# Retention attention and a SwiGLU block on one core: which queue stores the weight sums, and where their first groups stand

## The chip, the cores and the metric

The kernel runs on one core of one Trainium2 chip. The time is device time in microseconds for one execution of the whole program; the number for a kernel is the median of its runs. Engines are named as the profile names them: PE (TensorE), DVE (VectorE), ACT (ScalarE), POOL (GpSimd) and SP (SyncE). SP here only issues DMAs; ACT and POOL issue some as well, and an issuing engine spends time on each issue.

## The reference

```python
# retention attention: B=8, H=8, S=576, D=64, float32
scores = scale * np.matmul(q, k.transpose(0, 1, 3, 2))
gamma = 1.0 - 2.0 ** (-5.0 - np.arange(H, dtype=np.float32))
Dmat = np.where(rel >= 0, gamma[:, None, None] ** rel[None, :, :], 0.0)
attn = np.matmul(scores * Dmat[None, :, :, :], v)
# (B,H,S,D) -> x of 4608 tokens x 512
# SwiGLU: w_gate, w_val 512 x 1536, w_out 1536 x 512
g = x @ w_gate
out = (g * (1.0 / (1.0 + np.exp(-g))) * (x @ w_val)) @ w_out
```

## The kernel before

**Attention.** The 32 pairs of heads (`load`, `tick`) are worked through one after the other. `load(i)` fetches q, k (L282) and k, v (L287) of a pair, and `tick` computes its retention chunk by chunk, with a running state: DVE transposes qk to qT and kT (L492), ACT scales kn (L507) and qk (L489), PE multiplies (L532 to L573), ACT copies the results out (L584, L626, L656), and DVE applies the decay (L580, L590 to L608). A load is issued on SP into a rotating buffer, so its first issue waits until DVE has read the former contents (kT, L492). One pair, number 11, goes to a buffer of its own and is issued on ACT's DMA queue. Ticks are put in between the matmuls of the feed-forward part.

**Feed-forward.** The tokens are worked in tiles. The first 512 tokens (tile 0) go through plain matmuls: `up0` (L853 and L864 are its matmuls and those of `down0`; L856 takes silu on ACT, L857 multiplies on DVE), then `down0`, then `out0` (L870 stores the result). All later tiles (`up_stage(n)`, then down steps) use fast products: sums of blocks of x and of the weights are multiplied in fewer matmuls, and the products are added up again. L1183 is the matmul of the up half, L1374 that of the down half; every addition of two operands goes through one helper at L1040, on DVE or POOL; `finish` takes silu on ACT (L1197) and multiplies on DVE or POOL (L1198). The d_ff columns are taken in three quarters `qd` (NQ = 3), and each has seven sets of weights, in the order 1, 2, 6, 7, 4, 5, 3.

**Weight rounding.** The weights arrive as 64-bit numbers. ACT (L389, L390) splits them and DVE (L406, L407) puts them together to float32, half a block of columns after the other, while `up0` runs; ACT issues the loads of the next raw weights (L372).

**Weight sums for the up half.** In the stage n = 1 the sums of each set are made once. `w_sets(qd)` returns the sums (`outer_sums`, `inner_sums`, both on POOL) and `store`. The sums `new[o]` (128 partitions x 1024 float32, 512 KB) lie in one of three blocks of SBUF: sets 7 and 3 share the first, 6 and 2 the second, 1, 4 and 5 the third. PE multiplies with them there in stage 1, and they are stored to DRAM (`up_sets`, L1116) so that later tiles can fetch them. There are 21 such stores: three in `early_sums` (quarter 0, sets 1, 2 and 7, emitted in the `down0` loop), the others in `up_stage(1)`, each a few slots behind its sums. The sums of the next set of a block wait until its store has landed. The raw halves of each set are stored by SP (L1118 and L1119).

**Weight sums for the down half.** `out_sums(qd)` makes 26 sums per quarter, in groups of three stores (L954, on SP, 128 KB each). Quarters 0 and 1 are summed on POOL (L886) in six places of SBUF, which come free when a store has landed; quarter 2 on DVE. `negate(qd)` (L916, ACT) goes ahead of the first group of a quarter. Later tiles fetch these sums (L995).

**The order.** Every engine runs its instructions in the order in which the program emits them. Around the change the order is written out by hand: a list `plan` (L1442 onward) holds the calls for `up0(f)`, f = 2 to 11, and what is put between them. Behind f = 7, 10 and 11 stands `next_load(t)` (L1462), which loads the pair that is AHEAD pairs later: load(10), load(11) and so on. Behind it the groups of `out_sums` are put, by the dictionary in L1463, up to f = 7, 10 and 11. The remaining groups follow in the `down0` loop, one after each `down0(f)`. In the built program the DMAs that SP and ACT issue use eight completion semaphores in turn; each issue waits until the earlier DMA that used its semaphore has landed, whichever of the two engines issued that. POOL's DMAs have semaphores of their own.

Of the kernel before, what the change touches and what calls it, by code (L numbers as in the profile page):

```python
# [131 lines left out]
def kernel(  # L132
# [32 lines left out]
    nc = tc.nc  # L165
# [4 lines left out]
    P = 128  # L170
# [671 lines left out]
    def up0(f, chunks):  # L842

        pair = banks[2 * (f % 2) : 2 * (f % 2) + 2]
        for gv, bank in enumerate(pair):
            for c in chunks:
                w = w_up[:, f // 4, gv, f % 4, c // 2, (c % 2) * P : (c % 2 + 1) * P]
                if f == 2 or f == 3 and gv == 0:
                    for m in range(2):
                        nc.tensor.matmul(bank[:, ts(m, TB)], w, xs[0][:, c, ts(m, TB)],  # L850
                                         start=(c == 0 and m == 0), stop=(c == HP - 1), skip_group_check=True)
                    continue
                nc.tensor.matmul(bank, w, xs[0][:, c, :], start=(c == 0), stop=(c == HP - 1))  # L853
        if HP - 1 in chunks:
            s = io[:, (f % 2) * T0 : (f % 2 + 1) * T0]
            nc.scalar.activation(out=s, in_=pair[0], func=AF.Silu)  # L856
            nc.vector.tensor_tensor(out=hid0[f], in0=pair[1], in1=s, op=ALU.mult)  # L857
# [56 lines left out]
    def negate(qd):  # L914
        for n, s in enumerate((3, 5)):
            nc.scalar.mul(out=negatives[2 * qd + n], in_=w_dn[:, qd, s // 2, s % 2], mul=-1.0)  # L916
# [122 lines left out]
    def combine(eng, out, a, b, sign):  # L1039
        eng.tensor_tensor(out=out, in0=a, in1=b, op=ALU.add if sign > 0 else ALU.subtract)  # L1040
# [53 lines left out]
    def w_sets(qd):  # L1094

        up = lambda n, k: w_up[:, qd, :, 2 * n : 2 * n + 2, k, :]
        sets = {1: up(0, 0), 2: up(0, 1), 7: up(1, 0), 3: up(1, 1), 5: hid[:, qd, 2:4, 0:2], 6: hid[:, qd, 0:2, 2:4], 4: hid[:, qd, 2:4, 2:4]}
        blocks = (rest[:, x0_at + 1024 : x0_at + 2048], extra_at(1536, 1024), extra_at(0, 1024))
        new = {o: blocks[b].rearrange("p (g j x) -> p g j x", g=2, j=4) for o, b in {6: 1, 1: 2, 7: 0, 4: 2, 2: 1, 5: 2, 3: 0}.items()}

        def outer_sums(o):
            out, a, b = {5: (5, 7, 1), 6: (6, 3, 5), 7: (7, 3, 7), 4: (4, 2, 6)}[o]
            return [lambda g=g: combine(nc.gpsimd, sets[out][:, g], sets[a][:, g], sets[b][:, g], -1) for g in range(2)]

        def inner_sums(o):
            z = lambda k, m: sets[o][:, :, m, k * P : (k + 1) * P]
            to = lambda j: new[o][:, :, j]
            return [lambda: combine(nc.gpsimd, to(1), z(0, 1), z(0, 0), -1),
                    lambda: combine(nc.gpsimd, to(0), z(1, 1), z(0, 1), -1),
                    lambda: combine(nc.gpsimd, to(2), z(1, 1), to(1), -1),  # L1110
                    lambda: combine(nc.gpsimd, to(3), z(1, 0), to(2), -1)]

        def store(o, new_ones):
            dst = up_sets[qd][SETS.index(o)]
            if new_ones:
                return [lambda: nc.gpsimd.dma_start(out=dst[:, 6 * P :], in_=new[o].rearrange("p g j x -> p (g j x)"))]  # L1116
            raw = dst[:, 0 : 6 * P].rearrange("p (g x) -> p g x", g=2)
            return [lambda: nc.sync.dma_start(out=raw[:, :, P:], in_=sets[o][:, :, 0]),  # L1118
                    lambda: nc.sync.dma_start(out=raw[:, :, 0:P], in_=sets[o][:, :, 1, P:])]  # L1119

        return sets, new, outer_sums, inner_sums, store
# [313 lines left out]
    def next_load(t):  # L1435
        if t + AHEAD < NP:
            load(t + AHEAD)
# [6 lines left out]
    def round_until(i):  # L1444
        while todo and order.index(i) >= todo[0]:
            m = todo.pop(0)
            plan.extend(lambda j=j: rounding(j) for j in (2 * m, 2 * m + 1))
# [4 lines left out]
    for f in range(2, NF):  # L1452
        round_until({4: 12, 6: 13, 8: 14, 9: 15, 10: 16, 11: 17}.get(f, f + 2))
        plan.append(lambda f=f: up0(f, range(HP)))
        if f - 1 in tick_at and f < 7:
            plan.append(lambda t=tick_at[f - 1]: next_load(t))
        if f in tick_at and f > 2:
            plan.append(lambda t=tick_at[f]: tick(t, HP, FIRST))
            if tick_at[f] == HP + 1:
                plan.append(end_transposes)  # L1460
        if f in (7, 10, 11):
            plan.append(lambda t=tick_at[f]: next_load(t))  # L1462
        for _ in range({7: 3, 10: 4, 11: 3}.get(f, 0)):  # L1463
            if f >= (7, 10, NF)[groups[0][0]]:
                if f + 1 == NF and more_places:
                    plan.append(lambda places=more_places[:4]: pool_places.extend(places))
                    more_places.clear()
                if len(groups) % 9 == 0:
                    plan.append(lambda qd=groups[0][0]: negate(qd))
                plan.append(lambda group=groups.pop(0)[1]: group())  # L1470
# [87 lines left out]
```

## Time and profile before

| | |
|---|---|
| median of 3 runs | 1034.03 us (1033.91 to 1036.57) |
| profiled execution | 1034.89 us, its span 1033.2 us |
| granted TensorE clock, mean | 0.997 |
| busy | PE 1009.1, DVE 727.6, POOL 557.4, ACT 286.7 us |
| up sums stored by POOL (L1116) | 15 + 6 stores of 512 KB |
| down sums stored by SP (L954) | 78 stores of 128 KB |
| 40 slices of 25.8 us | PE at 9 tenths or more in all but the first (6), the sixth and tenth (8) and the last (8) |

A row of the timeline gives the start in us from the beginning of the span, the duration of the merged run, engine, line, operation, what is written and read, the number of instructions, and in brackets how long the engine had been idle before it and who ended that. Rows of ACTq and SPq are DMA issues, with the time that they kept the issuing sequencer. In the window view each engine's busy time in a stretch stands beside the granted clock.

### The profile page before, as it was taken

Reading aid. Unit: us, or ns where it says so; the run is one execution under the profiler, and the core shown is the slowest. Engines: PE = TensorE matmul, PEld = TensorE weight load, DVE = VectorE, ACT = ScalarE, POOL = GpSimd, SP = SyncE. Lnnn points to the kernel's source line nnn. Section 1 sums busy time; section 2 is a strip of 40 time slices with the busy share of each in tenths; the row PEclk is TensorE's granted clock in tenths of the full one; section 3 lists DMA queues with packets and bytes.
Section 4 is the critical chain, followed back from the end, with each engine's and each line's share of the span. In section 5 each row is a group of like instructions: output and inputs, shape, how many; then the busy total and the mean of one; then the engine's idle time right before and its main releaser. Section 6 shows DMA issues by size and latency. Waiting matters only on the chain.

```text
span 1033.2 us, 21382 instructions
## 1 busy us (share of the span) xinstructions
PE 1009.1 (98%) x8356; PEld 828.7 (80%) x8356; DVE 727.6 (70%) x1212; ACT 286.7 (28%) x638; POOL 557.4 (54%) x603
## 2 busy tenths in 40 slices
PE   6999989998999999999999999999999999999998
PEld 4644445887888888888888888888888888888887
DVE  5488878587788766875768768858576668565744
ACT  4465532131242231123333111133220012333110
POOL 3402259867474216764657237765582486566625
PEclk9999999999999999999999999999999999999999
DMA  9999887856595887756558777443454554445553
GB/s 242 251 263 248 216 198 264 262 147 191 116 260 159 203 237 197 208 178 181 166 163 234 197 187 218 163 144 143 143 189 154 159 162 163 154 142 182 177 162 102
DMA packets 281612, 194.38 MB, mean 188 GB/s; under 512 B 212968, under 2 KB 251112, under 8 KB 281512
## 3 DMA queue, kind: packets, MB, share of 16 engines
q1 hardware_dynamic: 244088, 82.51, 32.9%
q10 hardware_dynamic: 33760, 99.10, 29.2%
q0 software_dynamic: 3664, 11.41, 3.0%
q8 instruction: 66, 1.08, 0.5%
q14 instruction: 34, 0.28, 0.1%
HBM read 154.04 MB, written 38.93 MB: 187 GB/s over the span
## 4 chain that ended last, share of the span: by engine, by line
PE 82%; DMA 7%; DVE 5%; SPq 2%; issue 1%; ACT 1%; POOL 1%; ACTq 0%; DVEq 0%; POOLq 0%
PE bankE L1183 11%; PE bankA L1183 11%; PE bankB L1183 10%; PE bankC L1183 10%; PE bankB L1374 7%; PE bankC L1374 7%; PE bankE L1374 7%; PE bankA L1374 6%; DVE rest L1040 2%; PE outer L1183 2%; PE inner L1183 2%; PE outer L532 1%; DMA v<-in_v_dram 1%; PE outer L559 1%; DMA dn<-rest 1%
## 5 line engine op out<-in xcount | busy, mean ns | idle before, releaser
L1040 POOL TENSOR_TENSOR rest<-rest 128x512 f32<-128x512 f32 (+1 forms) x141 | 150.4, 1078 | 156.6 <-DVE rest L1040 114.2
L1198 POOL TENSOR_TENSOR arena<-rest,io 128x256 f32<-128x256 f32 x144 | 105.7, 745 | 73.2 <-ACT io L1197 72.9
L1197 ACT ACTIVATE io<-rest 128x256 f32<-128x256 f32 x192 | 79.4, 417 | 219.6 <-DVE rest L1040 159.2
L1183 PE MATMUL bankA<-rest,arena 128*128 128x256 f32 x416 | 107.6, 384 | 4.1 <-DVE rest L1040 3.9
L1183 PE MATMUL bankB<-rest,arena 128*128 128x256 f32 x416 | 106.1, 380 | 0.1
L1040 DVE TENSOR_TENSOR rest<-bankB,rest 128x512 f32<-128x512 f32 x113 | 76.1, 682 | 38.5 <-PE bankB L1183 24.6
L1183 PE MATMUL bankE<-rest,arena 128*128 128x256 f32 x400 | 102.2, 380 | 0.3 <-issue 0.3
L1040 DVE TENSOR_TENSOR rest<-bankA,rest 128x512 f32<-128x512 f32 x106 | 71.5, 682 | 40.6 <-PE bankA L1183 21.0
L1040 DVE TENSOR_TENSOR rest<-bankE,rest 128x512 f32<-128x512 f32 x105 | 71.0, 684 | 38.7 <-PE bankE L1183 25.8
L1040 POOL TENSOR_TENSOR arena<-arena 128x256 f32<-128x256 f32 (+1 forms) x84 | 76.3, 929 | 34.7 <-PE bankC L1183 19.6
L1183 PE MATMUL bankC<-rest,arena 128*128 128x256 f32 x372 | 94.8, 380 | 0.1
L1183 PEld LDWEIGHTS bankA<-rest,arena 128*128 128x128 f32 x416 | 78.8, 191 | 17.1 <-issue 3.4
L1040 DVE TENSOR_TENSOR rest<-bankC,rest 128x512 f32<-128x512 f32 x103 | 69.7, 683 | 30.1 <-PE bankC L1183 12.6
L1183 PEld LDWEIGHTS bankB<-rest,arena 128*128 128x128 f32 x416 | 78.8, 190 | 11.6 <-DVE rest L1040 0.9
L1183 PEld LDWEIGHTS bankE<-rest,arena 128*128 128x128 f32 x400 | 75.3, 190 | 11.8 <-DVE rest L1040 0.8
L1183 PEld LDWEIGHTS bankC<-rest,arena 128*128 128x128 f32 x372 | 70.1, 190 | 10.8 <-DVE rest L1040 1.2
L886 POOL TENSOR_TENSOR rest<-rest 128x256 f32<-128x256 f32 x43 | 34.3, 822 | 74.3 <-DVE rest L407 38.8
L1374 PE MATMUL bankB<-arena 128*128 128x256 f32 x264 | 61.0, 381 | 0.0
L1374 PE MATMUL bankC<-arena 128*128 128x256 f32 x264 | 60.8, 380 | 0.0
L1374 PEld LDWEIGHTS bankC<-arena 128*128 128x128 f32 x264 | 50.0, 190 | 6.9
L1374 PEld LDWEIGHTS bankB<-arena 128*128 128x128 f32 x264 | 49.8, 190 | 6.9
L1374 PE MATMUL bankA<-arena 128*128 128x256 f32 x240 | 55.3, 380 | 0.0
(267 smaller groups left out, 1930.1 us busy)
## 6 DMA issues: line engine op xcount, KB each, us to landing
arena<-up ACTq DMA_DIRECT2D x63, 896.0 KB, 4.6
arena<-dn ACTq DMA_DIRECT2D x65, 384.0 KB, 3.7
arena<-dn SPq DMA_DIRECT2D x39, 384.0 KB, 3.4
dn<-rest SPq DMA_DIRECT2D x78, 128.0 KB, 1.8
out_dram<-rest SPq DMA_DIRECT2D x35, 256.0 KB, 3.1
qk<-in_q_dram SPq DMA_DIRECT2D x108, 72.0 KB, 2.8
qk<-in_k_dram SPq DMA_DIRECT2D x108, 72.0 KB, 3.5
up<-arena POOLq DMA_DIRECT2D x15, 512.0 KB, 4.3
```

The costliest lines, as they stand in the source:

```text
L532: m = nc.tensor.matmul(value(i, hl, c), s["v"][rows, at], ret[rows, c % 2 if whole(i) else hl, c // 2], start=start, stop=start, skip_grou ...
L559: nc.tensor.matmul(xr[half[hl]] if c + 1 == NC else value(i, hl, c), state[half[hl], c, :], s["qT"][half[hl], ts(c, L)], start=False, stop ...
L886: eng.tensor_tensor(out=dst, in0=srcs[0], in1=srcs[1], op=ALU.add if op[0] == "add" else ALU.subtract)
L1040: eng.tensor_tensor(out=out, in0=a, in1=b, op=ALU.add if sign > 0 else ALU.subtract)
L1183: m = nc.tensor.matmul(b[:, g * TB : (g + 1) * TB], w[:, g], x, start=(opens and g == 0), stop=True, skip_group_check=True)
L1197: nc.scalar.activation(out=s, in_=src[:, 0:TB], func=AF.Silu)
L1198: (nc.vector if busy else nc.gpsimd).tensor_tensor(out=hid[:, qd, 2 * H + h, 2 * T + t], in0=src[:, TB : 2 * TB], in1=s, op=ALU.mult)
L1374: nc.tensor.matmul(b[:, m * TB : (m + 1) * TB], lhs[:, qd, ts(m, P)], w[:, qd], start=(opens and qd == 0 and m == 0), stop=(qd == NQ - 1), ...
```

## The change

The store of the new sums is issued by SP in place of POOL, and the first three groups of `out_sums(0)` are emitted behind f = 10 in place of f = 7. There they stand behind `next_load` of that place, and so on SP's queue behind load(10); the fourth to seventh group follow them as before, and the last three stay behind f = 11. `negate(0)` moves with its group. The order of PE's and DVE's instructions stays as it was; on POOL the 21 issues are gone, and on SP they stand between the loads and stores.

```diff
@@ -1113,7 +1113,7 @@
             dst = up_sets[qd][SETS.index(o)]
             if new_ones:
-                return [lambda: nc.gpsimd.dma_start(out=dst[:, 6 * P :], in_=new[o].rearrange("p g j x -> p (g j x)"))]
+                return [lambda: nc.sync.dma_start(out=dst[:, 6 * P :], in_=new[o].rearrange("p g j x -> p (g j x)"))]
@@ -1460,7 +1460,7 @@
         if f in (7, 10, 11):
             plan.append(lambda t=tick_at[f]: next_load(t))
-        for _ in range({7: 3, 10: 4, 11: 3}.get(f, 0)):
+        for _ in range({10: 7, 11: 3}.get(f, 0)):
```

## The prediction

> **What bounds the kernel now.** First the page: the busy shares, the chain's shares and the issue row of the moved stores.
>
> ```profile
> PE 1009.1 (98%) x8356; PEld 828.7 (80%) x8356; DVE 727.6 (70%) x1212; ACT 286.7 (28%) x638; POOL 557.4 (54%) x603
> PE 82%; DMA 7%; DVE 5%; SPq 2%; issue 1%; ACT 1%; POOL 1%; ACTq 0%; DVEq 0%; POOLq 0%
> up<-arena POOLq DMA_DIRECT2D x15, 512.0 KB, 4.3
> ```
>
> TensorE is the bound: 1009.1 of 1033.2 us. Neither edit changes a matmul, so a gain can only come from PE's 24 us of idle time and from matmuls at a low granted clock. By 52 us windows PE idles 9 us before 52 us (load time, untouched), 1.8 in 52–104, 3.75 in 104–156, 3.07 in 208–260, 1.6 in 260–312 and nearly nothing later. So I read PE's timeline for the gaps inside the region that the edits touch:
>
> ```profile
> 104.85 1.55 PE L853 MATMUL bankA<-rest,arena 128*128 128x512 f32 x3 [1.52 <-ACT io L856]
> 142.80 0.70 PE L532 MATMUL outer<-ret,v 64*64 64x64 f32 x16 [2.65 <-ACT rest L626]
> 146.47 0.27 PE L567 MATMUL outer<-qT,kT 64*64 64x64 f32 x2 [0.25 <-DVE kT L492]
> 245.19 2.04 PE L1183 MATMUL bankA<-rest,arena 128*128 128x256 f32 x4 [3.07 <-DVE rest L1040]
> ```
>
> The bracket is the idle time and who ended it. Two of these cost more than they show: in the windows 140–150 and 240–250 the granted clock is 0.83 against 1.00 in the neighbours. Edit 1 (groups behind the load) can touch the first three, edit 2 (stores on SyncE) the last.
>
> **Edit 1, step by step.** The gap at 142.80 is traced back on ACT and SP:
>
> ```profile
> 125.64 4.63 ACTq L282 DMA_DIRECT2D rest<-in_q_dram  x3
> 130.31 2.47 ACTq L282 DMA_DIRECT2D rest<-in_k_dram  x4
> 133.74 0.39 ACTq L287 DMA_DIRECT2D kn<-in_k_dram  x1
> 138.87 0.39 ACTq L287 DMA_DIRECT2D v<-in_v_dram  x1
> 139.31 0.72 ACT L916 ACTIVATE rest<-rest 128x256 f32<-128x256 f32 x2 [13.53 <-DMA dn<-rest]
> 139.94 0.35 ACT L584 COPY even<-inner 128x256 f32<-128x256 f32 x1
> ```
>
> ```profile
> 118.28 8.27 SPq L954 DMA_DIRECT2D dn<-rest  x9
> 126.65 2.05 SPq L282 DMA_DIRECT2D qk<-in_q_dram  x4
> 132.84 5.76 SPq L954 DMA_DIRECT2D dn<-rest  x5
> ```
>
> ACT issues load(11) itself. Its DMAs and SP's share eight completion semaphores in turn, so each issue waits until an earlier DMA of either queue has landed. On SP nine stores of down weight sums (8.27 us) stand ahead of load(10); load(10)'s v lands at 138.6, just before ACT's last issue at 138.87. Only then do L916, L584 and L626 run, and PE gets its operands at 142.75.
>
> After: the nine stores stand behind load(10). Its first issue then waits for the previous kT, which DVE ends at 122.17, so it goes some 126.65 − 122.2 = 4.5 us earlier and its last DMA lands near 132. ACT's last issue now waits for a store of the first group that stands behind the load; I place that store's landing at 135.3 to 137.5 (issue at 128.6, 0.5 to 0.9 us per store, 1.8 us to land). L584 then starts at 136.3 to 138.2 in place of 139.94: 1.6 to 3.6 us earlier.
>
> What is at stake on PE: an undisturbed tick took 130.76 to 133.02, 2.26 us; this one ended at 147.20, with PE free from 140.15, so the ideal end is 142.41 and the stall costs 4.79 us (2.65 and 0.25 idle, 1.89 of matmuls at low clock). If ACT comes 2.8 us earlier (the late half of my span, since a queue seldom runs at its best) PE gains **2.8**; ends 0 (another store holds ACT as long) and 4.79. What is late next is kT on DVE.
>
> The groups' sums move too. Now POOL's L886 (97.64, four in 3.68 us) lies on DVE's L406 and L407 at 98.3 to 101.8, which take 0.95–1.10 us there against 0.41 and 0.69 just after: 0.43+1.10+0.95+1.00 against 2×(0.41+0.69), 1.28 us late in the chain DVE, ACT L389/L390, ACT L856, which ends PE's gap of 1.52. After, the sums lie at 118.5 to 122.4, where DVE does tick work, and the roundings of 122.08 to 125.6, slowed alike today, are free as well. Gain **1.2** (ends 0 and 1.52).
>
> Given back: the nine stores' first moves from 118.28 to about 128.6, but SP issues the other 69 from 132.84 on at half a microsecond each and ends at 178.86; I expect 176.5 to 180.6, so the sums' POOL work is not later by more than 1.7. The four out stores (178.97) go behind a moved up store near 182.5; DVE overwrites their source from 187.92 and may wait 1–2 us. Cost **0.5** (0 to 1). L916 moves from 96.35 to ACT's gap at 118: two instructions of 0.36, hidden in idle time; ACT there is 28% busy; without cover 0.7.
>
> Edit 1: −2.8 −1.2 +0.5 = **−3.5** (−6.3 to +1.0).
>
> **Edit 2.** Off POOL go 21 issues, each 0.58 with 0.30 before it (the row below): 18.5 us on an engine that is 54% busy. Its sums lead PE by more than 9 us except at 193–196 (0.35–0.6 us), so this alone is worth nothing at PE. It acts through DVE:
>
> ```profile
> 219.23 0.41 DVE L1198 TENSOR_TENSOR arena<-rest,io 128x256 f32<-128x256 f32 x1
> 238.45 5.06 DVE L1198 TENSOR_TENSOR arena<-rest,io 128x256 f32<-128x256 f32 x1
> 243.44 0.68 DVE L1040 TENSOR_TENSOR rest<-bankB,rest 128x512 f32<-128x512 f32 x1
> ```
>
> ```profile
> 238.09 0.58 POOL L1116 DMA_DIRECT2D up<-arena  x1 [0.30 <-POOL arena L1040]
> 238.69 2.50 POOL L1040 TENSOR_TENSOR arena<-arena 128x512 f32<-128x512 f32 x2
> ```
>
> L1198 takes 0.41 us while POOL idles and 5.06 while POOL sums run; L1040 behind it ends the wait of PE at 245.19. POOL's run there starts on PE at 224.07 with one store at 231.70 and one at 238.09 in it: without them it ends 1.76 us earlier, at about 242.3, then waits for a block. L1198 should end near 241.8, so of PE's 3.07 us 1.7 go. In 289–305 L1198 takes 2.86, 2.67, 2.42 and 1.40; POOL's run from 279.36 again ends 1.8 us earlier, but PE idles only 0.46 there: I count 0.3. Together **−2.0**. Ends: −3.07−0.46−1.5 (low clock of 245–249) = −5.0; and +5.0, below.
>
> On SP the 21 stores join a queue whose loads wait for kT. Followed through the built program: up1_6 moves from 231.7 to 239, behind the load that SP starts at 231.62; up1_2, 5 and 3 from 256–264 to 266–267.5; up2_1 from 293.4 to 301.7, landing near 309, which the sums of up2_4 (now 300.3) wait for. Those have 9 us and more before PE. Three late stores land at 325.5 to 328.5, and ACT's L995 fetch into their blocks (323.33, 327.06) waits 2 to 2.7 us, ahead of L1197. Its data land at 328.2, needed at 337.26: 9.06 of slack; L1197's consumers have about 2.5. Loads go at most 5 us later (eleven issues of 0.5) and lead by 15 or more. Cost 0, up to **+0.3** taken (0 to 2).
>
> The Trainium skill, "SBUF — State Buffer", section "SBUF: two separate sides", says that a VectorE operation with two SBUF inputs and a GpSimd operation exclude each other on a shared port pair for one whole instruction. By that rule L1198 would wait for one POOL sum, about 1.3 us, and edit 2's gain would be near 0; the row's 5.06 is longer than several, so the row is used.
>
> The Trainium skill, "DMA: Bandwidth & Descriptors", section "SWDGE vs HWDGE vs iDMA", says that GpSimd's DMAs and the others feed different queues of the DMA engines, between which these alternate. That speaks against the edit: the half-megabyte stores would now stand in one line with the loads. By it a load behind a store could land up to 4.3 us (the page row of the profile) later; it would still be early.
>
> **Sum.** −3.5 −2.0 +0.3 = −5.2 against the profiled execution's 1034.89 (span 1033.2 plus 1.7): 1029.7. The median shown is 0.86 lower, so in its frame 1034.03 − 5.2 = **1029**.
>
> **Rivals.**
> - *Only edit 1 pays*, 1034.03 − 3.5 = 1030.5. For it: L1198's place in POOL's run may just shift. Against: POOL loses 0.88 us at each issue. 0.15.
> - *ACT is held as long as before*: the store of the first group that its last issue waits for lands near 138.6, after a slow queue. Then only the 1.2 at 104.85 is left: 1033, no difference to be measured. For it: three ACT issues took 4.63 us at 125.64. 0.13.
> - *Slower: POOL without pauses locks DVE out.* For it: L1198 gets in where POOL pauses, and the 0.88 us at each of 21 issues are such pauses. Place: the sums runs of quarters 1 and 2, PE waiting on DVE rest L1040 as at 245.19. Price: in each of the two runs L1198 waits out another piece, about 2.5 us (2.50, 2.67, 2.86 above), with DVE without slack: 5 us, 1039 if edit 1 pays nothing at the same time. It decides where L1198 of 238.45 ends later than now, 243.5. Against: it started inside an issue's pause and did not profit from it. 0.22.
> - *Both pay in full*: −6.3 −5.0 +0.3 = −11, 1023. Both low-clock stretches would have to go. 0.08.
>
> **How the numbers follow.** The forecast has 0.42. Range: 1023 (both in full) to 1039 (the slower case's price); about half of that case and little of the best lies outside, some 0.14. What this kernel's measurement can tell is 0.3%, 3.1 us. Faster: 0.42 + 0.15 + 0.08 = 0.65; same 0.13; slower 0.22.
>
> **What would show it.** Right: PE's gap at 142.80 shrinks to under 1 us and ACT's last load issue goes before 138; the gap at 104.85 is under 0.5; the gap near 245 is under 1.6, with POOL's run ended at about 242.3; TensorE's clock is 0.9 or more in 140–150. Wrong: ACT still waits 13 us ahead of L584; new waits of POOL or ACT on up stores that reach PE between 245 and 345; a gap of PE on DVE rest L1040 longer than 3.07. A PE gap near 188–196 would mean that the out stores cost more than 0.5.

## The result, and the profile after

The changed kernel took 1027.03 us (1025.09 to 1029.28, 10 runs) against 1034.11 (1027.78 to 1038.49, 10 runs) for the one before: ratio 0.9936, 95% interval 0.9917 to 0.9956. That is 7.1 us less; 5 were forecast. Two more measurements of it gave 0.9922 (0.9894 to 0.995) and 0.9957 (0.9938 to 0.9976).

The page of the changed kernel, with the same rows as for before:

```profile
PE 1006.6 (98%) x8356; PEld 827.5 (81%) x8356; DVE 708.1 (69%) x1212; ACT 286.3 (28%) x638; POOL 545.4 (53%) x582
PE 81%; DMA 8%; DVE 4%; SPq 3%; issue 2%; ACT 2%; POOL 1%; ACTq 0%; DVEq 0%
up<-arena SPq DMA_DIRECT2D x15, 512.0 KB, 3.9
```

POOL lost its 21 issues and 12 us of busy time, and DVE, which runs the same 1212 instructions, is busy 19.5 us less: its instructions got shorter. PE's gaps in its timeline from 90 to 270 us are these and no others:

```profile
138.55 0.46 PE L532 MATMUL outer<-ret,v 64*64 64x64 f32 x16 [0.76 <-ACT rest L626]
142.69 0.27 PE L567 MATMUL outer<-qT,kT 64*64 64x64 f32 x2 [1.79 <-DVE kT L492]
177.53 1.99 PE L1183 MATMUL bankB<-x_odd,arena 128*128 128x256 f32 x8 [0.49 <-ACT rest L869]
```

The gaps near 105 and 245 are gone. The one at the tick is as long as before (2.55 against 2.90) but has another end: kT on DVE. The clock is 1.00 in 140–150 and in 240–250. A small new gap stands where `out0` begins.

PE's order is the same in both kernels, so I laid the two traces over each other matmul by matmul. The changed execution gains 1.70 us near 105. At the tick it gains 3.1 and gives 1.4 back, net 1.73. It loses 0.65 near 181, gains 3.0 at the gap of 245, 1.5 by the clock behind it and 1.0 around 308, and loses 0.7 near 439. Read alone, this pair of profiles confirms both halves of the prediction. The experiments show that it doesn't: one half of it is luck of the execution.

DVE and POOL ahead of the gap that is gone, in the changed kernel's timelines:

```profile
233.90 1.42 DVE L1198 TENSOR_TENSOR arena<-rest,io 128x256 f32<-128x256 f32 x1
235.84 0.89 DVE L1198 TENSOR_TENSOR arena<-rest,io 128x256 f32<-128x256 f32 x1
```

```profile
221.23 15.21 POOL L1040 TENSOR_TENSOR arena<-arena 128x512 f32<-128x512 f32 x15 [5.22 <-issue]
```

POOL now runs fifteen sums with no issue in between, and L1198 still gets in, within 1.42 us. Fewer pauses did not lock DVE out.

### The profile page after: what moved, and what is told of

It reads as the page before. It is cut to its first block, busy times and chain, and to the rows that moved or that the text cites. A ratio compares the mean times of both kernels' runs of the same rounds, so it can differ in the third digit from the quotient of the medians.

```text
span 1025.8 us, 21376 instructions
## 1 busy us (share of the span) xinstructions
PE 1006.6 (98%) x8356; PEld 827.5 (81%) x8356; DVE 708.1 (69%) x1212; ACT 286.3 (28%) x638; POOL 545.4 (53%) x582
## 4 chain that ended last, share of the span: by engine, by line
PE 81%; DMA 8%; DVE 4%; SPq 3%; issue 2%; ACT 2%; POOL 1%; ACTq 0%; DVEq 0%
PE bankE L1183 12%; PE bankB L1183 11%; PE bankA L1183 11%; PE bankC L1183 11%; PE bankB L1374 7%; PE bankC L1374 7%; PE bankE L1374 7%; PE bankA L1374 6%; PE outer L1183 2%; PE inner L1183 2%; DMA kn<-in_k_dram 2%; DMA v<-in_v_dram 1%; DMA dn<-rest 1%; PE outer L532 1%; DVE rest L1040 1%
## 5 line engine op out<-in xcount | busy, mean ns | idle before, releaser
L1040 POOL TENSOR_TENSOR rest<-rest 128x512 f32<-128x512 f32 (+1 forms) x141 | 151.4, 1085 | 156.6 <-DVE rest L1040 114.2
L1198 POOL TENSOR_TENSOR arena<-rest,io 128x256 f32<-128x256 f32 x144 | 106.0, 748 | 73.1 <-ACT io L1197 72.7
L1197 ACT ACTIVATE io<-rest 128x256 f32<-128x256 f32 x192 | 79.4, 417 | 214.3 <-DVE rest L1040 147.1
L1040 DVE TENSOR_TENSOR rest<-bankA,rest 128x512 f32<-128x512 f32 x106 | 71.8, 685 | 51.1 <-PE bankA L1183 24.2
L1040 DVE TENSOR_TENSOR rest<-bankB,rest 128x512 f32<-128x512 f32 x113 | 76.4, 685 | 38.4 <-PE bankB L1183 22.8
L1040 POOL TENSOR_TENSOR arena<-arena 128x256 f32<-128x256 f32 (+1 forms) x84 | 76.0, 932 | 41.5 <-DMA up<-arena 20.2
L1040 DVE TENSOR_TENSOR rest<-bankE,rest 128x512 f32<-128x512 f32 x105 | 71.3, 686 | 38.1 <-PE bankE L1183 26.2
L1040 DVE TENSOR_TENSOR rest<-bankC,rest 128x512 f32<-128x512 f32 x103 | 69.8, 685 | 30.5 <-PE bankC L1183 14.5
```

The costliest lines, as they stand in the source:

```text
L1197: nc.scalar.activation(out=s, in_=src[:, 0:TB], func=AF.Silu)
L1198: (nc.vector if busy else nc.gpsimd).tensor_tensor(out=hid[:, qd, 2 * H + h, 2 * T + t], in0=src[:, TB : 2 * TB], in1=s, op=ALU.mult)
```

## The experiments

My theory after the first comparison was A: the edits act apart, the groups for some 2.8 us, the stores for the rest. The rival B: the gap near 245 goes because the groups' edit shifts POOL against PE. I undid each edit.

**Only the stores.**

```diff
-        for _ in range({10: 7, 11: 3}.get(f, 0)):
+        for _ in range({7: 3, 10: 4, 11: 3}.get(f, 0)):
```

> Only the stores go to SyncE; the groups stay where they were before. Theory A (the two edits act apart: the stores' share is the 5.4 us that PE wins between 240 and 312 us, less 0.6 us given back): about 1029.3 us, 0.9955 of before; PE's gaps near 105 (1.5 us) and 143 (2.6 us) are there as before, the one near 245 is under 1 us. Theory B (the gap near 245 goes only because the groups' edit brings PE and VectorE there 3 to 4 us earlier relative to GpSimd): about 1034 us, 1.000, and the gap near 245 is still 2 us or more.

Measured 1024.68 us, 0.9943 (0.9923 to 0.9963); a repeat, below, gave the same ratio. No gap near 245: B is out. But A said that the gaps near 105 and 143 would stay, and both are gone too, although up to POOL's first store (175.12 us in the profile of before) this program is that of the kernel before.

**Only the groups.**

```diff
-                return [lambda: nc.sync.dma_start(out=dst[:, 6 * P :], in_=new[o].rearrange("p g j x -> p (g j x)"))]
+                return [lambda: nc.gpsimd.dma_start(out=dst[:, 6 * P :], in_=new[o].rearrange("p g j x -> p (g j x)"))]
```

> Only the groups move; the stores stay on GpSimd. Theory A: the groups' share is 1.7 us at the gap near 105, 1.7 us at the attention tick near 142, less some 0.6 us near 180, so about 1031.3 us, 0.9973 of before, and PE's gap near 245 of about 3 us is there, some 3 us earlier. Theory B: about 1027 us, the gap near 245 is gone.

Measured 1036.12 us against 1030.9: 1.0045 (1.0027 to 1.0062), slower. Theory A fell on its first half: alone, the groups' edit gains nothing. In the profile the gap near 105 is gone, the tick still has gaps of 1.03 and 1.33, and the gap of 3.07 stands at 242.

**A second profile of the kernel before.**

> The kernel before once more, for a second profile. In the run with only the stores moved, PE's gap near 105 was gone and the one near 143 nearly so, though the program up to 178 us is that of the kernel before there. Theory A (those two gaps belong to the order of the groups): they are here again, 1.5 and 2.6 us. Theory C (they come of slow transfers in the one execution that was profiled): at least one of them is smaller by over 1 us, and the gap near 245 of about 3 us, which the stores' edit removes, is here again.

1032.08 us, 0.9994 (0.9974 to 1.0014). Its PE timeline:

```profile
105.04 3.70 PE L853 MATMUL bankA<-rest,arena 128*128 128x512 f32 x8 [1.69 <-ACT io L856]
142.70 0.46 PE L532 MATMUL outer<-ret,v 64*64 64x64 f32 x16 [2.42 <-ACT rest L626]
247.32 1.10 PE L1183 MATMUL bankA<-rest,arena 128*128 128x256 f32 x4 [3.08 <-DVE rest L1040]
```

By its wording this supports A: all three gaps are there. But the execution that was profiled was the slowest of its twelve (1035.54), as the first profile of before (1034.89) was above its median. Six profiles in this study have the groups in their old place. These two have the gap near 105 and the other four don't; at the tick three of the four still issue load(11) on ACT, and none of these has more than 0.84 us at kT. So the same order gives both pictures.

What differs between them is when transfers land. For the gap near 105 the chain begins at ACT's L507, which waits for a k transfer; L916 behind it releases POOL's sums. The first row is from the profile of before, the second from only-the-stores:

```profile
95.48 0.96 ACT L507 ACTIVATE kn<-kn,tab 128x256 f32<-128x256 f32 x2 [3.94 <-DMA kn<-in_k_dram]
92.55 0.96 ACT L507 ACTIVATE kn<-kn,tab 128x256 f32<-128x256 f32 x2 [2.27 <-DMA kn<-in_k_dram]
```

L916 began at 96.35 and 96.57 in the two profiles of before, and at 90.89 to 93.42 in the other four; the sums were then over, or nearly so, when the roundings began.

At the tick, ACT's last issue of load(11) went like this in only-the-stores:

```profile
133.13 0.39 ACTq L287 DMA_DIRECT2D v<-in_v_dram  x1
133.56 0.72 ACT L916 ACTIVATE rest<-rest 128x256 f32<-128x256 f32 x2 [9.51 <-DMA rest<-in_k_dram]
134.19 0.35 ACT L584 COPY even<-inner 128x256 f32<-128x256 f32 x1
```

and in the changed kernel:

```profile
134.62 0.39 ACTq L287 DMA_DIRECT2D v<-in_v_dram  x1
135.06 0.72 ACT L916 ACTIVATE rest<-rest 128x256 f32<-128x256 f32 x2 [11.44 <-DMA dn<-rest]
135.69 0.35 ACT L584 COPY even<-inner 128x256 f32<-128x256 f32 x1
```

In the old order L584 can start at 134.19, earlier than in the new. There the last issue waits for ACT's own fourth k transfer, which took 4.0 us to land in this execution and 6.4 us in both profiles of before, on top of a late start (132.47 in the first of them, against 129.16). In the new order it waits for a down store behind load(10). In six of seven profiles of the new order in which ACT issues the pair, PE then waits 1.3 to 1.9 us for kT; the five such profiles of the old order showed 0.84 at most (0.25 and 0.81 in those of before).

**Only the groups, again.**

> Only the groups moved, once more, for a second profile: its first profile was the fastest of its executions and 4 us under their median, so it didn't show what costs. Theory: 1.003 to 1.006 of before again, and this profile shows, beside the gap of 3 us near 242, a stall of PE of 2 us or more that the first did not. Rival: it was that chip, and the ratio is within 0.9985 to 1.0015.

1036.07 us, 1.002 (1.000 to 1.0039), between the two expectations. From PE's timeline:

```profile
243.26 2.04 PE L1183 MATMUL bankA<-rest,arena 128*128 128x256 f32 x4 [3.08 <-DVE rest L1040]
285.49 1.13 PE L1183 MATMUL bankA<-x_odd,arena 128*128 128x256 f32 x4 [2.03 <-issue]
```

The expected further stall is at 285, 2.03 against 1.1 to 1.2 in both profiles of before, and the granted clock was lower behind two gaps: 0.66 in 240–250 (0.83 and 1.00 in the profiles of before) and 0.84 in 280–290 (1.00 in both). In 140–150 it was 0.83 (0.83 and 0.68). Both ratios are above 1, by 0.2 and 0.45%. What PE waited for at 285 the profile doesn't name, and a kernel below that gained, load(11) on GpSimd, has a wait of 1.88 near that place. So what the edit costs alone, and why nothing beside the stores, isn't settled.

**Two of the 21 stores** (before, with one line changed).

```diff
-                return [lambda: nc.gpsimd.dma_start(out=dst[:, 6 * P :], in_=new[o].rearrange("p g j x -> p (g j x)"))]
+                return [lambda: (nc.sync if qd == 1 and o in (6, 1) else nc.gpsimd).dma_start(out=dst[:, 6 * P :], in_=new[o].rearrange("p g j x -> p (g j x)"))]
```

> The kernel before with two of the 21 stores moved to SyncE, those of sets 6 and 1 of quarter 1, which GpSimd issued at 231.7 and 238.1 us in the midst of the sums that end ahead of the gap near 245. Theory A: the gap goes (under 1 us) and with it the low clock behind it: 0.9955 to 0.997 of before, the larger part of the whole gain. Rival: the gap stays over 2 us, since it hangs on when the blocks come free or on the other 19 stores: 0.999 to 1.001.

1027.45 us against 1031.78: 0.9954 (0.9931 to 0.9977), and no gap near 245. These two issues carry some 4 of the 6 us that all 21 stores gain, though the two intervals overlap.

**Tiny issues added** to the changed kernel, 4 bytes of each of 128 partitions, issued by GpSimd where it had issued a store (`marks` are new tensors in DRAM).

```diff
-                return [lambda: nc.sync.dma_start(out=dst[:, 6 * P :], in_=new[o].rearrange("p g j x -> p (g j x)"))]
+                return [lambda: nc.sync.dma_start(out=dst[:, 6 * P :], in_=new[o].rearrange("p g j x -> p (g j x)")), lambda: nc.gpsimd.dma_start(out=marks[len(SETS) * qd + SETS.index(o)], in_=new[o][:, 0, 0, 0:1])]
```

> As the changed kernel, and GpSimd issues in addition, where it stored the sums before, a store of 4 bytes per partition. GpSimd thus has the issue times and pauses of before, while the large stores stay on SyncE. Theory A1 (what the stores' edit wins is the time of the issues on GpSimd, which holds VectorE's multiplies L1198 behind its sums): 1030 to 1032 us, a gap of PE on L1040 of 2 us or more near 240. Theory A2 (it is the traffic and the waits for landings that changed, not GpSimd's time): 1027 us as the changed kernel, and no such gap.

1081.11 us, 1.0473 (1.0446 to 1.05). Neither theory: I had taken such a store for nearly free. From the view of the DMA issues, and PE's longest wait:

```profile
qk<-in_q_dram SPq DMA_DIRECT2D x108, 72.0 KB, 4.4
mark<-arena POOLq DMA_DIRECT2D x15, 0.5 KB, 9.9
```

```profile
371.40 3.66 PE L1183 MATMUL bankE<-rest,arena 128*128 128x256 f32 x8 [26.23 <-DVE rest L1040]
```

A store of half a kilobyte took 10 us to land, and what was in flight with it was late as well (q loads: median 4.4 us, against 3.0 in the changed kernel). Blocks came free late, SyncE's queue stood, and ACT's L1197 behind an L995 fetch waited 31.6 us. So this run can't tell A1 from A2; it tells something else, below.

**GpSimd's time without a transfer**: the changed kernel with six memsets of an unused tile in the two places.

```diff
-                return [lambda: nc.sync.dma_start(out=dst[:, 6 * P :], in_=new[o].rearrange("p g j x -> p (g j x)"))]
+                return [lambda: nc.sync.dma_start(out=dst[:, 6 * P :], in_=new[o].rearrange("p g j x -> p (g j x)"))] + [lambda: nc.gpsimd.memset(ident, 0.0)] * (6 if qd == 1 and o in (6, 1) else 0)
```

> The changed kernel with six short memsets on GpSimd at each of the two places where it issued the stores of sets 6 and 1 of quarter 1 (they write a tile that is not used any more), some 0.9 us each: GpSimd's time there as before, without any transfer. Theory A1 (the two issues matter by the time that they take from GpSimd's run, so that L1198 meets it at another point): the gap of some 3 us near 240 is back, and 3 to 5 us are lost against the changed kernel, 0.996 to 0.998 of before. Theory A3 (it is the issue itself, the writing of descriptors, that holds VectorE off): no gap, 0.992 to 0.994.

1026.59 us, 0.9952 (0.9937 to 0.9967), between the two expectations; the gap decides, and there is none near 245. POOL and DVE there:

```profile
235.24 1.51 POOL L1116 MEMSET ident<- 128x128 f32 x6
```

```profile
235.48 0.41 DVE L1198 TENSOR_TENSOR arena<-rest,io 128x256 f32<-128x256 f32 x1
```

Six memsets took 1.5 us, more than the 0.88 of an issue, so POOL's run was delayed by more than in the kernel before, and the gap did not come back: A1 is out. L1198 began inside the memsets and took 0.41. In the kernel before, L1198 at 238.45 began inside an issue (238.09 to 238.67) and took 5.06. That is A3: the issue, not its time.

I then counted over the traces. In the eight profiles without stores issued by POOL among its sums (three of the changed kernel, two of the stores alone, the memsets, and the two kernels with moved loads below) all 8 x 48 L1198 on DVE took at most 1.72 us. Those of 0.6 us or more ended 0.3 us behind the POOL sum in which they began, also where POOL's next sum followed at once (five that began in the last 0.05 us of a sum ended behind the next). In the six profiles with such issues, six to eight L1198 in each took 1.8 to 5.07. Of 27 that began while an issue ran, 24 took 1.39 us or more. The 5.06 or 5.07 is in all four profiles of kernels that had the two issues and the gap, each time 0.36 us behind the issue's start.

The traces also show where such a hold ends. Each of the 41 L1198 of 1.8 us or more ended 0.28 to 0.29 us behind a POOL sum that was followed by a pause of 0.08 us or more; L1198 stayed out for up to five sums that followed each other at once. In the kernel before, the first such pause behind the issue of 238.09 was at 243.22. The tiny issues do the same, so the half megabyte of the store isn't needed for it:

```profile
294.62 0.56 POOL L1116 DMA_DIRECT2D mark<-rest  x1
295.20 4.93 POOL L1040 TENSOR_TENSOR arena<-arena 128x512 f32<-128x512 f32 x4
295.54 4.88 DVE L1198 TENSOR_TENSOR arena<-rest,io 128x256 f32<-128x256 f32 x1
```

**Load(11) on SyncE** (changed kernel; L260 gives `nc.sync` for every pair) and **load(11) on GpSimd** (stores on SyncE, groups in the old place).

```diff
-        queue = nc.scalar if i == needed(1) - 3 else nc.sync
+        queue = nc.gpsimd if i == needed(1) - 3 else nc.sync
```

> As the changed kernel, but the loads of the attention pair that ScalarE issues go on SyncE. If ScalarE's waits at these issues still hold the tick (11.4 us ahead of L916 in the changed kernel), the gaps of 0.76 and 1.79 us near 138 and 142 go: about 1024.5 us, 0.9907 of before. Rival: the tick is held by VectorE's own work ahead of kT, or the pair arrives late behind the stores: 1027 us or more, with a gap of PE near 142 or at the next tick.

> Stores on SyncE, groups in their old place, and the loads of the one pair that ScalarE issues go on GpSimd, which is idle then. If ScalarE's waits at these issues are what makes the tick near 140 late in some executions, ScalarE runs L584 some 3 us earlier, the tick's gaps are under 0.3 us, the executions lie closer together, and the time is 1 to 3 us below the kernel with the stores alone: 0.990 to 0.993 of before. Rival: the ten issues of 0.6 us hold back the down sums on GpSimd and so the end of the down part near 178: no better than the stores alone.

0.9981 (0.9966 to 0.9996) and 0.9965 (0.9949 to 0.9981): no better than the changed kernel. The first part of each expectation held: ACT ran L584 at 131.73 and 131.50 and the tick's gaps were gone. The rivals' part decided. On SyncE the pair came late and pushed the down stores back:

```profile
153.79 0.69 PE L543 MATMUL inner<-v,kn 64*64 64x64 f32 x32 [1.98 <-DMA v<-in_v_dram]
179.53 2.70 PE L1183 MATMUL bankB<-x_odd,arena 128*128 128x256 f32 x8 [2.05 <-ACT rest L869]
```

On GpSimd the gap behind the down stores was 0.16 and 1.24. What was won at the tick was lost at `out0`, whose L869 waits for down stores to land, and on SyncE at the next tick as well.

**Stores alone and both edits, on one chip.**

> Only the stores moved, once more, on the chip of the changed kernel's third run. 0.993 to 0.996 of before. If moving the groups pays beside the stores, the changed kernel is 1 us or more below this one; if it costs, as it did alone, this one is 1 us or more below; else the two edits come to the same and the groups' share is nil.

> The changed kernel, third time, beside the kernel with the stores alone: 0.992 to 0.994 of before by its two earlier ratios.

1025.40 us, 0.9943 (0.9925 to 0.996), and 1026.77 us, 0.9957 (0.9938 to 0.9976), the second a little above what was expected.

> The changed kernel once more, on the chip of the next two. 0.993 to 0.995 of before; no gap of PE near 240. If the groups' edit costs time when it stands alone (1.0045) and not here, its cost lies in something that the stores' edit also changes.

That second run of the changed kernel gave 1026.92 us, 0.9922, with two gaps of 0.90 on ACT rest L869 at 179 and 184. Means of ratios: 0.9938 with both edits, 0.9943 with the stores alone. The groups' share beside the stores is nil within some 2 us. No version was measurably below the changed kernel.

## Why the prediction was right, and where it was not

- **The sum held, its split did not.** Forecast: −3.5 for the groups, −1.7 for the stores with SyncE's cost. Measured: between no effect and +4.6 for the groups (1.0045, 1.002, and nil beside the stores), about −6 for the stores (0.9943 twice). The two errors had opposite signs, so it is in part luck that 5 was near 7.1.
- **The gap at 105** (−1.2) rested on POOL's sums lying on DVE's roundings. They do so in both profiles of before. In the stores alone the same sums, in the same order, ran from 93.90 to 97.50 and the roundings from 97.05 on took 0.72 once and then 0.42 and 0.69: no gap. The chain was read rightly; that it belongs to the order alone was inferred from one execution. It also took a k transfer that landed late, ahead of L507.
- **The tick** (−2.8): the step that failed is that the nine down stores ahead of load(10) make ACT's last issue late. With the stores ahead, ACT's issue went at 133.07 to 134.50 in three profiles and at 138.77 and 138.87 in those of before; with them behind, at 133.91 to 137.23 in seven. The late ones came of slow landings. The prediction set load(10)'s v, landed at 138.6, beside the issue of 138.87; what released the issue was ACT's own fourth k transfer, landed at 138.85. "What is late next is kT" held, with 1.3 to 1.9 us of gap that I had not priced.
- **Given back at out0** (0.5): 0.65 in the first profile, about 2 in the second. The cause named, the moved out stores, was not the one seen: ACT L869 waited for down stores to land.
- **The stores** (−2.0): place and chain were right, L1198 behind POOL ahead of L1040 and PE at 245. The size was wrong, 1.7 of 3.07 with the low clock left out, since I took L1198 to be freed by POOL ending earlier. What goes is the whole long hold: 3.0 us of gap and 1.5 of clock in the overlay.
- **The rule on the shared port pair** was set aside for the row of 5.06. The row is true of sums behind an issue; the rule (at most one GpSimd instruction) fits every L1198 where GpSimd issues no stores: 1.72 at most. The Trainium skill, "SBUF — State Buffer", section "Who interferes with whom", adds that a VectorE instruction with two SBUF inputs contends with a GpSimd instruction that reads SBUF, not with one that only writes it; L1198's 0.41 inside the memsets agrees.
- **The slower rival** had the mechanism upside down: an issue in POOL's run is no door for L1198, it is what shuts it out. That L1198 gets in where POOL pauses held for the sums behind an issue; without issues it needs no pause.
- **SyncE's queue** (0 to 0.3): POOL waited up to 9.07 us for a block (at 299.17), ACT's and POOL's new waits reached no gap of PE named after them. Right.

## What to carry to other kernels

One profile is one execution: before a gap is given to an order of instructions, look whether a program with the same order shows it too, and where the profiled execution lies among the runs (before: 1027.8 to 1038.5). When two engines share something, ask what lies between their instructions as well as how long they take: here two DMA issues of 0.58 us on GpSimd cost VectorE a 5 us hold and TensorE 4 us. A duration many times its undisturbed length (5.06 against 0.41) on the chain of waits is the row to experiment on first.

## What was not expected of the hardware

- With DMA issues of GpSimd among its sums, a VectorE multiply with two SBUF inputs was held for up to 5.07 us, over several GpSimd instructions and until GpSimd first paused (41 of 41 holds of 1.8 us or more); without them it was never over 1.72 (384 instances). Why an issue lengthens the hold past the next sum isn't shown.
- A store of 4 bytes from each of 128 partitions landed after 7.9 to 15.2 us; many loads and stores that flew with it took 8 to 15 us. Twenty-one of them cost 54 us.
